# Local attention scores with a block diagonal of keys in four column tiles, and row steps queued one task later

## The chip, the core and the metric

The kernel runs on one core of a Trainium2 chip. A core has TensorE (matrix products, PE in the profile, with its weight loads listed apart as PEld), VectorE (DVE), ScalarE (ACT), GpSimd (POOL) and SyncE (SP), and 16 DMA engines. The metric is the device time of one execution in microseconds; a kernel's time is the median of its runs.

## What is computed

A masked attention over 8 batches of 8 heads, 576 positions, 64 channels, followed by a mixture of 8 experts of which each token uses one. The first four heads see the last 32 positions (local), the others every 32nd position (strided).

```python
mask_local = (rel >= 0) & (rel < stride)
mask_strided = (rel >= 0) & (pos[None, :] % stride == pos[:, None] % stride)
scores = np.where(masks[None, :, :, :], scores, -1000000000.0)
attn = softmax(scores)                      # over the last axis
x = (attn @ v).transpose(0, 2, 1, 3).reshape(B * S, H * D)
expert = argmax(x @ w_gate); gate = softmax(x @ w_gate)[expert]
out = gate * (relu(x @ w1[expert]) @ w2[expert])
```

## The kernel before

**Attention.** Each batch is cut into five tasks (`BANK_PAIRS`), 40 in all. A task fills one PSUM bank of 128x512 scores. Tasks 0 and 1 of a batch hold the local scores of two heads each, for 16 blocks of 32 queries; tasks 2 to 4 hold the rest of the local scores and the strided ones. `stage_s` writes a mask into the bank by a matmul with the identity (line 403), adds the scores (lines 411, 419, 424), and `softmax` runs over the bank on VectorE, ScalarE and GpSimd (lines 352 to 362). Three tasks later `stage_t` transposes the probabilities (line 453), and four tasks later `av_local` (line 478) and `av_strided` (line 467) multiply them with the values; ScalarE copies the results to `xT` (line 162).

**Local scores.** A block of 32 queries of two heads meets 64 keys. Before, the queries stand as a block diagonal in `qkl` (head 0 in rows 0 to 63, head 1 in rows 64 to 127, zeros between). `wide` takes the 64 columns of a block as the weights, with a step of 16 elements, and 64 keys as the moving side; the result is 64 rows of 64 columns, and two column tiles are used in turn:

```python
q = qkl[k][:, 0:2 * LQ].rearrange("p (q j) -> p q j", j=LB)
nc.tensor.matmul(sb[64 * i:64 * i + 64, col:col + 64], q[:, :, j], qkl[k][:, k0:k0 + 64],
                 start=False, stop=last, tile_position=(0, 64 * i))
```

Every fp32 matmul of the program is two instructions in the trace, each with a weight load of its own.

**Row steps.** When a batch's last values are made, `row_steps` lists what follows for its rows: the logits of three row tiles at a time (`logits`: line 528, a copy `ls` to SBUF on VectorE at line 158, transposes at line 535, small work on VectorE), the rows' transposes and their store to DRAM (`xrows`, line 520), and after every second batch the routing (`route`). The list goes into `queue`, and `step()` takes one piece; an iteration of the task loop calls `step()` four times, twice ahead of `stage_s` and twice behind the values. `row_steps` puts one empty piece (`pause`) ahead of the logits.

**Early experts.** After the fourth batch's routing, `fillers()` starts windows of 256 rows of experts 0, 2, 4 and 6; `filling()` takes one piece of them twice in an iteration. A window gathers its rows (line 239), transposes them (line 275), splits weights into a high and a low part (ScalarE line 222, VectorE line 223) and multiplies (lines 297 to 299, 286 to 288). What is left of them comes behind the loop. Then the eight experts follow, with three small remainders (`small`, lines 1031 and 1043) whose matmuls have 32 columns of weights, 128 moving columns and four column tiles.

**What sets the order.** On TensorE the order is the program's own (`manual_schedule`). On the other engines a scheduler sets it from priorities. Loads of queries, keys and values are issued by SyncE, in its order, when the buffer is free; a local task's `qkl` has one buffer, freed when the scores of the batch before are done.

Of the kernel before, what the change touches and what calls it, by code (L numbers as in the profile page):

```python
# [22 lines left out]
QB = 32  # L23
# [93 lines left out]
def host_constants(np):  # L117
# [3 lines left out]
    for p in range(128):  # L121
        q = p % QB
        m[p, 0, q + 1:q + QB + 1] = 0.0
        m[p, 1, max(q + 1, QB if p < 2 * QB else 0):q + QB + 1] = 0.0
# [19 lines left out]
def moe_attn(ctx, tc, qk, vv, wg, wcat, blob0, blob, out):  # L144
# [175 lines left out]
    with ExitStack() as actx:  # L320
# [13 lines left out]
        def make_masks():  # L334
            for k, kinds in enumerate((((0, 1, 1), (1, 8, 0)), ((0, 2, 0), (2, 8, 2)), ((0, 8, 2),))):
# [31 lines left out]
        qkl = [loc.tile([128, 2 * LQ + LK], F32, name=f"qkl{k}") for k in range(2)]  # L367
        pTl = [loc.tile([128, 2, 512], F32, name=f"pTl{k}") for k in range(2)]
        for k in range(2):
            nc.vector.memset(qkl[k][64:128, 0:LQ], 0.0)  # L370
            nc.gpsimd.memset(qkl[k][0:64, LQ:2 * LQ], 0.0)
# [4 lines left out]
        def load_qk(i):  # L376
            if i < len(tasks):
                b, k = tasks[i]
                if k < 2:
                    o = QKO[k]  # L380
                    nc.sync.dma_start(out=qkl[k][64:128, LQ:], in_=qk[b, 64:128, o:o + LQ + LK])
                    nc.sync.dma_start(out=qkl[k][0:64, 0:LQ], in_=qk[b, 0:64, o:o + LQ])
                    nc.sync.dma_start(out=qkl[k][0:64, 2 * LQ:], in_=qk[b, 0:64, o + LQ:o + LQ + LK])
                    return
# [15 lines left out]
        def stage_s(b, k):  # L400
# [7 lines left out]
            def wide(j, i, col, last):  # L408
                q = qkl[k][:, 0:2 * LQ].rearrange("p (q j) -> p q j", j=LB)
                k0 = 2 * LQ + QB * j  # L410
                nc.tensor.matmul(sb[64 * i:64 * i + 64, col:col + 64], q[:, :, j], qkl[k][:, k0:k0 + 64],  # L411
                                 start=False, stop=last, tile_position=(0, 64 * i))
# [14 lines left out]
            for n, (kind, hp, m) in enumerate(BANK_PAIRS[k]):  # L427
                for y in range(2):
                    col = 128 * n + 64 * y
                    last = n == 3 and y == 1  # L430
                    if kind == "l":
                        for i in range(2):
                            wide(4 * m + 2 * i + y, i, col, last)
                    elif kind == "lx":
# [34 lines left out]
        def av_local(b, xT, off):  # L469
            for hp in range(2):  # L470
                av = bank("v")
                for m in range(4):
                    for i in range(2):
                        n = 2 * m + i
                        vt = v_of(b, hp, "l", n)
# [320 lines left out]
        def row_steps(g, bb, xT, L):  # L796
# [422 lines left out]
```

## Time and profile before

| | us |
|---|---|
| median of three runs | 666.14 |
| lowest, highest | 664.89, 667.58 |
| profiled execution | 671.04 |
| its span on the core | 668.8 |

The rows of the section below come from that profiled execution; times are from the span's start. In a row by stretch, each engine's busy time is followed by the number of its instructions in brackets, then come the granted clock of TensorE as a share, the mean busy share of the DMA engines, and GB/s. A row of a group gives the line, the engine, the operation, output<-inputs, shapes, the count, the busy time, and the mean of one in ns. A row of the timeline gives start, length, engine, line and count, and in square brackets the idle time ahead of it with what ended it. Matmuls are pipelined: the time from the start of one group to the start of the next is what it holds TensorE, the busy time of one is longer by its tail.

### The profile page before, as it was taken

The numbers are of one execution on the slowest core, as the hardware profiler recorded it, in microseconds if no ns is written. First come the engines' busy times: TensorE is split into PE (matmuls) and PEld (weight loads), VectorE is DVE, ScalarE is ACT, GpSimd is POOL, SyncE is SP. The second block draws the span as 40 slices with busy tenths as digits, with TensorE's granted clock in tenths as the row PEclk, the third lists the DMA queues.
The fourth block names the chain that finished last, engine by engine and source line by source line (L and its number), as shares of the span: only waits on it lengthen the run. The fifth ranks groups of instructions, "written<-read, shape, count | busy, mean of one in ns | idle before, by whom it ended". The sixth has DMA issues, their size and how long they took to land.

```text
span 668.8 us, 14979 instructions
## 1 busy us (share of the span) xinstructions
PE 626.7 (94%) x6136; PEld 522.0 (78%) x6154; DVE 400.9 (60%) x788; ACT 327.3 (49%) x584; POOL 148.1 (22%) x168
## 2 busy tenths in 40 slices
PE   4999889789979999999899899999999999999996
PEld 3877778577858778888588788887898788887885
DVE  5667968656757369899424576823596235863332
ACT  1556665565645565356332555622565224753232
POOL 3232223420041021216100413200612004301021
PEclk9899999989989999899999999999999999999999
DMA  9968998994652865558933576872896546863301
GB/s 283 243 231 270 299 302 256 333 342 162 222 212 96 300 225 167 179 193 280 384 142 117 204 292 209 282 252 92 314 356 219 170 181 225 328 238 150 126 20 64
DMA packets 36550, 149.85 MB, mean 224 GB/s; under 512 B 5114, under 2 KB 5504, under 8 KB 26240
## 3 DMA queue, kind: packets, MB, share of 16 engines
q1 hardware_dynamic: 22848, 105.92, 47.1%
q10 hardware_dynamic: 7344, 22.70, 9.5%
q0 software_dynamic: 6288, 20.26, 8.3%
q8 instruction: 49, 0.80, 0.5%
q14 instruction: 21, 0.17, 0.1%
HBM read 129.69 MB, written 19.63 MB: 223 GB/s over the span
## 4 chain that ended last, share of the span: by engine, by line
PE 35%; issue 34%; POOL 7%; DMA 5%; DVE 4%; ACT 2%; POOLq 1%; ACTq 0%; another core or an unknown queue 0%
POOL xg L239 4%; PE t L297 4%; PE t L299 4%; PE t L298 4%; PE y L286 4%; PE y L287 3%; PE y L288 3%; POOL out_dram L258 2%; PE s L411 2%; DMA raw<-in_wcat_dram 1%; PE v L520 1%; DMA out_dram<-y,oids 1%; PE v L467 1%; DMA xg<-xd,eids 1%; DMA xd<-xr 1%
## 5 line engine op out<-in xcount | busy, mean ns | idle before, releaser
L223 DVE TENSOR_TENSOR wlo<-raw,whi 128x1024 fp32r<-128x1024 f32 x136 | 164.0, 1222 | 76.2 <-ACT whi L222 68.1
L222 ACT CAST whi<-raw 128x1024 fp32r<-128x1024 f32 x136 | 139.3, 1051 | 63.4 <-PE s L288 25.4
L297 PE MATMUL t<-xh,whi 128*128 128x256 f32 (+1 forms) x384 | 126.9, 332 | 2.3 <-ACT xh L231 2.1
L298 PE MATMUL t<-xl,whi 128*128 128x256 f32 (+1 forms) x384 | 124.3, 324 | 0.0
L299 PE MATMUL t<-xh,wlo 128*128 128x256 f32 (+1 forms) x384 | 123.6, 322 | 0.5 <-DVE wlo L223 0.5
L303 DVE SCALAR_TENSOR_TENSOR hl<-t,hh 128x256 fp32r<-128x256 f32 (+1 forms) x96 | 49.0, 510 | 103.2 <-ACT hh L302 102.9
L302 ACT ACTIVATE hh<-t 128x256 fp32r<-128x256 f32 (+1 forms) x96 | 43.8, 456 | 120.7 <-PE t L299 109.2
L297 PEld LDWEIGHTS t<-xh,whi 128*128 128x128 f32 x384 | 73.1, 191 | 13.3 <-ACT xh L231 3.3
L286 PE MATMUL y<-whi,hh 128*128 128x512 f32 x192 | 77.2, 402 | 2.1 <-ACT hh L302 2.1
L299 PEld LDWEIGHTS t<-xh,wlo 128*128 128x128 f32 x384 | 73.6, 192 | 6.3 <-DVE wlo L223 1.1
L298 PEld LDWEIGHTS t<-xl,whi 128*128 128x128 f32 x384 | 73.4, 191 | 5.9 <-DVE xl L232 0.3
L287 PE MATMUL y<-wlo,hh 128*128 128x512 f32 x192 | 75.9, 395 | 0.0
L288 PE MATMUL y<-whi,hl 128*128 128x512 f32 x192 | 74.6, 395 | 0.0
L362 POOL TENSOR_TENSOR prob<-prob,ri 128x512 f32<-128x512 f32 x40 | 42.5, 1063 | 122.9 <-DVE ri L361 87.6
L258 POOL DMA_INDIRECT out_dram<-y,oids x24 | 27.5, 1147 | 115.7 <-DVE y L257 110.9
L162 ACT COPY xT<-v 128x270 f32<-128x270 f32 (+1 forms) x80 | 30.1, 480 | 28.8 <-PE v L467 12.3
L286 PEld LDWEIGHTS y<-whi,hh 128*128 128x128 f32 x192 | 36.4, 189 | 9.4 <-ACT hh L302 2.9
L288 PEld LDWEIGHTS y<-whi,hl 128*128 128x128 f32 x192 | 35.9, 189 | 9.1 <-DVE hl L303 1.3
L287 PEld LDWEIGHTS y<-wlo,hh 128*128 128x128 f32 x192 | 36.5, 190 | 5.0
L358 DVE TENSOR_REDUCE sm<-prob 128x8 f32<-128x512 f32 x40 | 27.3, 683 | 21.5 <-ACT prob L356 21.2
L352 DVE TENSOR_REDUCE nm<-s 128x8 f32<-128x512 f32 x40 | 27.3, 683 | 18.5 <-PE s L411 14.0
L239 POOL DMA_INDIRECT xg<-xd,ids x24 | 30.2, 1259 | 31.9 <-ACT xh L231 18.9
(219 smaller groups left out, 1056.7 us busy)
## 6 DMA issues: line engine op xcount, KB each, us to landing
raw<-in_wcat_dram SPq DMA_DIRECT2D x68, 1024.0 KB
sraw<-in_wcat_dram ACTq DMA_DIRECT2D x12, 1024.0 KB
xd<-xr ACTq DMA_DIRECT2D x36, 264.0 KB
vl<-in_vv_dram SPq DMA_DIRECT2D x16, 512.0 KB
qkl<-in_qk_dram SPq DMA_DIRECT2D x16, 264.0 KB
vt<-in_vv_dram SPq DMA_DIRECT2D x16, 256.0 KB
qk<-in_qk_dram SPq DMA_DIRECT2D x8, 484.0 KB
qk<-in_qk_dram SPq DMA_DIRECT2D x8, 432.0 KB
```

The lines of the kernel that those rows point to most:

```text
L222: nc.scalar.copy(out=hi[:, sl], in_=raw[:, sl])
L223: i = nc.vector.tensor_tensor(out=lo[:, sl], in0=raw[:, sl], in1=hi[:, sl].bitcast(F32), op=ALU.subtract)
L239: lastp[0] = nc.gpsimd.indirect_dma_start(out=xg, out_offset=None, in_=xd[0:rows, :], in_offset=bass.IndirectOffsetOnAxis(ap=idc, axis=0))
L286: nc.tensor.matmul(yb[t], hh[:, ts], whi[:, w], start=(j == 0), stop=False)
L287: nc.tensor.matmul(yb[t], hh[:, ts], wlo[:, w], start=False, stop=False)
L288: nc.tensor.matmul(yb[t], hl[:, ts], whi[:, w], start=False, stop=(j == 7))
L297: nc.tensor.matmul(hb[:, 0:n], whi[:, w], xh[:, dc, :], start=(dc == 0), stop=False)
L298: nc.tensor.matmul(hb[:, 0:n], whi[:, w], xl[:, dc, :], start=False, stop=False)
L299: nc.tensor.matmul(hb[:, 0:n], wlo[:, w], xh[:, dc, :], start=False, stop=(dc == 3))
L302: nc.scalar.activation(out=hh[:, 0:n], in_=hb[:, 0:n], func=AF.Relu)
L303: nc.vector.scalar_tensor_tensor(out=hl[:, 0:n], in0=hb[:, 0:n], scalar=0.0, in1=hh[:, 0:n].bitcast(F32), op0=ALU.max, op1=ALU.subtract)
L362: lastp[0] = nc.gpsimd.tensor_tensor(out=pv, in0=pv, in1=ri.unsqueeze(2).broadcast_to([128, 8, 64]), op=ALU.mult)
```

## The change

Three things change.

- In `wide`, the 32 queries of both heads are the weights, as 32 contiguous columns, and the keys are the block diagonal on the moving side: two runs of 64. The result is 32 rows of 128 columns, written as two runs of 64 columns, in four column tiles. The mask, the loads into `qkl` and the host's layout follow it.
- Since the blocks stand in another order in the bank, `av_local` reads other columns of the probabilities and writes two runs of 32 columns in place of one of 64. It has as many matmuls as before.
- The list of `row_steps` goes into `late`, and from there into `queue` in the next task; the last batch's list goes into `queue` at once. The empty piece is gone.

```diff
-                    nc.sync.dma_start(out=qkl[k][64:128, LQ:], in_=qk[b, 64:128, o:o + LQ + LK])
-                    nc.sync.dma_start(out=qkl[k][0:64, 0:LQ], in_=qk[b, 0:64, o:o + LQ])
-                    nc.sync.dma_start(out=qkl[k][0:64, 2 * LQ:], in_=qk[b, 0:64, o + LQ:o + LQ + LK])
+                    nc.sync.dma_start(out=qkl[k][0:64, 0:LQ + LK], in_=qk[b, 0:64, o:o + LQ + LK])
+                    nc.sync.dma_start(out=qkl[k][64:128, 0:LQ], in_=qk[b, 64:128, o:o + LQ])
+                    nc.sync.dma_start(out=qkl[k][64:128, LQ + LK:], in_=qk[b, 64:128, o + LQ:o + LQ + LK])
...
-            def wide(j, i, col, last):
-                q = qkl[k][:, 0:2 * LQ].rearrange("p (q j) -> p q j", j=LB)
-                k0 = 2 * LQ + QB * j
-                nc.tensor.matmul(sb[64 * i:64 * i + 64, col:col + 64], q[:, :, j], qkl[k][:, k0:k0 + 64],
-                                 start=False, stop=last, tile_position=(0, 64 * i))
+            def wide(m, i, last):
+                j = 4 * m + i
+                keys = qkl[k][:, LQ:].rearrange("p (h x) -> p h x", h=2)[:, :, QB * j:QB * j + 64]
+                o = sb[QB * i:QB * i + QB, 256 * (m // 2):256 * (m // 2) + 256].rearrange("p (h y c) -> p h y c", h=2, y=2)
+                nc.tensor.matmul(o[:, :, m % 2], qkl[k][:, QB * j:QB * j + QB], keys,
+                                 start=False, stop=last, tile_position=(0, QB * i))
...
-                            c = 128 * m + 64 * i + 32 * h
-                            nc.tensor.matmul(av[64 * h:64 * h + 64, 64 * n:64 * n + 64], vt[:, 64 * h:64 * h + 64],
+                            c = 128 * (2 * m + h) + QB * i
+                            o = av[64 * h:64 * h + 64, 256 * m:256 * m + 256].rearrange("p (y r) -> p y r", y=2)
+                            nc.tensor.matmul(o[:, :, QB * i:QB * i + QB], vt[:, 64 * h:64 * h + 64],
                                              pTl[hp][:, :, c:c + QB], start=True, stop=True, tile_position=(0, 64 * h))
...
-            pause = [] if last else [single()]
-            steps = list(pause)
+            steps = []
             for r in range(3):
                 steps += [part(x) for x in lg]
-                if r == 0:
-                    steps += pause
...
-                    if k == 1:
+                    if k == 0:
+                        queue.extend(late)
+                        late.clear()
+                    elif k == 1:
...
-                        queue.extend(row_steps(g, bb, xTs[g], Ls[g]))
+                        (queue if b == B - 1 else late).extend(row_steps(g, bb, xTs[g], Ls[g]))
```

TensorE, from the last strided values of the second batch on. Before (a row is a run of equal instructions; `t` are transposed probabilities, `s` scores, `v` values, `y` the bank of logits and rows):

```order
L467 MATMUL v<-pT,vt 64x54 x20
L467 MATMUL v<-pT,vt 64x36 x4
L528 MATMUL y<-xT,wg_sb 32x384 x4
L453 MATMUL t<-cst_70,prob 128x128 x4
L528 MATMUL y<-xT,wg_sb 32x384 x4
L535 MATMUL y<-cst_70,ls 128x128 x3
L403 LDWEIGHTS identb
L403 MATMUL s<-mask_b,identb 128x512
L424 MATMUL s<-qk 54x54 x16
L535 MATMUL y<-cst_70,ls 128x128 x3
L453 MATMUL t<-cst_70,prob 128x128 x4
```

The same place of the changed kernel, whose lines stand two further down here (467 is 469, 528 is 530, 535 is 537):

```order
L469 MATMUL v<-pT,vt 64x54 x20
L469 MATMUL v<-pT,vt 64x36 x4
L455 MATMUL t<-cst_70,prob 128x128 x4
L403 LDWEIGHTS identb
L403 MATMUL s<-mask_b,identb 128x512
L425 MATMUL s<-qk 54x54 x16
L530 MATMUL y<-xT,wg_sb 32x384 x8
L455 MATMUL t<-cst_70,prob 128x128 x4
L537 MATMUL y<-cst_70,ls 128x128 x6
```

Both groups of logits moved behind the next task's transposes, mask and scores, and their transposes follow together.

SyncE, ahead of the first load of expert weights (`raw`), with the last loads of a batch in front of it. Before:

```order
L387 DMA qk<-in_qk_dram 128x864
L394 DMA vt<-in_vv_dram 128x512
L214 DMA raw<-in_wcat_dram 128x2048
L381 DMA qkl_135<-in_qk_dram 64x1056
L382 DMA qkl_135<-in_qk_dram 64x512
```

In the changed kernel, at the same place:

```order
L387 DMA qk<-in_qk_dram 128x864
L394 DMA vt<-in_vv_dram 128x512
L381 DMA qkl_135<-in_qk_dram 64x1056
L382 DMA qkl_135<-in_qk_dram 64x512
L383 DMA qkl_135<-in_qk_dram 64x544
L394 DMA vl<-in_vv_dram 128x1024
```

The load of weights moved behind the 14 loads of one more batch, of which the rows show the first four.

## Rows read from the trace of the kernel before

**Rows 1.** The page: busy time and share of the span by engine.

```profile
PE 626.7 (94%) x6136; PEld 522.0 (78%) x6154; DVE 400.9 (60%) x788; ACT 327.3 (49%) x584; POOL 148.1 (22%) x168
```

**Rows 2.** Busy time by stretch: PE, PEld, DVE, ACT, POOL, clock, DMA share, GB/s.

```profile
0.00:22.00 22.00, 13.20 (x183) 10.19 (x184) 11.41 (x33) 6.04 (x9) 7.67 (x15) 0.84 0.96 273
22.00:42.00 20.00, 19.02 (x384) 14.39 (x383) 14.90 (x37) 11.59 (x25) 6.63 (x9) 1.00 0.81 247
42.00:61.50 19.50, 18.96 (x389) 14.20 (x389) 12.91 (x33) 11.23 (x26) 5.31 (x6) 1.00 0.83 259
61.50:83.40 21.90, 20.11 (x417) 16.78 (x419) 19.39 (x57) 14.46 (x31) 6.14 (x11) 1.00 0.87 278
83.40:104.50 21.10, 19.14 (x391) 14.71 (x393) 14.34 (x36) 13.02 (x29) 5.39 (x8) 1.00 0.92 296
104.50:125.70 21.20, 19.23 (x416) 16.29 (x417) 17.92 (x59) 14.49 (x31) 6.85 (x12) 1.00 0.91 292
125.70:137.00 11.30, 7.54 (x113) 6.09 (x113) 4.01 (x14) 3.49 (x8) 6.57 (x9) 1.00 1.03 320
...
400.00:668.00 268.00, 263.49 (x1727) 220.59 (x1725) 133.68 (x169) 119.14 (x195) 49.80 (x41) 1.00 0.57 203
```

**Rows 3.** TensorE's matmuls grouped by line and shape.

```profile
L411 PE MATMUL s<-qkl 128*64 128x64 f32 x512 | 33.2, 289 | 2.7 <-DMA qkl<-in_qk_dram 1.6 <-issue 0.7
...
L478 PE MATMUL v<-pTl,vl 128*64 128x64 f32 x512 | 17.7, 223 | 1.9 <-issue 1.9
...
L1031 PE MATMUL v<-sraw,sxt 128*32 128x128 f32 x192 | 6.5, 276 | 0.0
...
L419 PE MATMUL s<-qk 64*32 64x64 f32 x128 | 3.4, 222 | 0.3 <-DMA xd<-xr 0.2
```

**Rows 4.** TensorE's weight loads grouped by line and shape.

```profile
L411 PEld LDWEIGHTS s<-qkl 128*64 128x64 f32 x512 | 30.8, 209 | 7.1 <-issue 6.5 <-DMA vl<-in_vv_dram 0.3 <-DMA qk<-in_qk_dram 0.3
...
L1031 PEld LDWEIGHTS v<-sraw,sxt 128*32 128x32 f32 x192 | 4.9, 109 | 2.1 <-issue 2.1
```

**Rows 5.** TensorE's timeline at the end of the second batch's values.

```profile
54.66 1.76 PE L528 MATMUL y<-xT,wg_sb 128*32 128x384 f32 x6
...
57.34 0.66 PE L453 MATMUL t<-cst,prob 128*128 128x128 f32 x4
57.93 0.85 PE L528 MATMUL y<-xT,wg_sb 128*32 128x384 f32 x8
58.71 0.55 PE L535 MATMUL y<-cst,ls 128*128 128x128 f32 x3
59.40 1.01 PE L424 MATMUL s<-qk 64*54 64x54 f32 x32
```

**Rows 6.** The same place after the first, third, fourth and fifth batch.

```profile
35.37 1.69 PE L528 MATMUL y<-xT,wg_sb 128*32 128x384 f32 x6
...
37.99 0.66 PE L453 MATMUL t<-cst,prob 128*128 128x128 f32 x4
...
79.03 2.16 PE L528 MATMUL y<-xT,wg_sb 128*32 128x384 f32 x8
81.83 0.55 PE L535 MATMUL y<-cst,ls 128*128 128x128 f32 x3 [0.65 <-DVE ls L158]
...
97.25 0.84 PE L528 MATMUL y<-xT,wg_sb 128*32 128x384 f32 x4
...
100.35 0.66 PE L453 MATMUL t<-cst,prob 128*128 128x128 f32 x4
...
122.59 1.37 PE L528 MATMUL v<-xT,wg_sb 128*32 128x384 f32 x8 [0.59 <-ACT xT L162]
```

**Rows 7.** Timeline: first scores, first load of expert weights, first expert matmul.

```profile
6.85 2.12 PE L411 MATMUL s<-qkl 128*64 128x64 f32 x32 [1.60 <-DMA qkl<-in_qk_dram]
...
83.19 0.33 SPq L214 DMA_DIRECT2D raw<-in_wcat_dram  x1
...
141.74 0.37 PE L297 MATMUL t<-xh,whi 128*128 128x256 f32 x1
```

More of the change, by code (lines that the diff above doesn't have):

```diff
@@ L123, in host_constants @@
         m[p, 0, q + 1:q + QB + 1] = 0.0
-        m[p, 1, max(q + 1, QB if p < 2 * QB else 0):q + QB + 1] = 0.0
+        m[p, 1, max(q + 1, QB if p < QB else 0):q + QB + 1] = 0.0
         r, a = divmod(p % 64, SR)
@@ L334, in make_masks @@
         def make_masks():
-            for k, kinds in enumerate((((0, 1, 1), (1, 8, 0)), ((0, 2, 0), (2, 8, 2)), ((0, 8, 2),))):
+            for k, kinds in enumerate((((0, 8, 0), (0, 1, 1), (2, 3, 1)), ((0, 2, 0), (2, 8, 2)), ((0, 8, 2),))):
                 for x0, x1, m in kinds:
@@ L365, in moe_attn @@
         loaded = {}
-        qkl = [loc.tile([128, 2 * LQ + LK], F32, name=f"qkl{k}") for k in range(2)]
+        qkl = [loc.tile([128, LQ + 2 * LK], F32, name=f"qkl{k}") for k in range(2)]
         pTl = [loc.tile([128, 2, 512], F32, name=f"pTl{k}") for k in range(2)]
         for k in range(2):
-            nc.vector.memset(qkl[k][64:128, 0:LQ], 0.0)
-            nc.gpsimd.memset(qkl[k][0:64, LQ:2 * LQ], 0.0)
+            nc.vector.memset(qkl[k][64:128, LQ:LQ + LK], 0.0)
+            nc.gpsimd.memset(qkl[k][0:64, LQ + LK:], 0.0)
         for k in range(2):
@@ L427, in stage_s @@
             for n, (kind, hp, m) in enumerate(BANK_PAIRS[k]):
+                if kind == "l":
+                    for i in range(4):
+                        wide(m, i, m == 3)
+                    continue
                 for y in range(2):
@@ L430, in stage_s @@
                     last = n == 3 and y == 1
[L431 to L434, printed above, removed]
+                    if kind == "lx":
                         for i in range(2):
@@ L471, in av_local @@
                 av = bank("v")
[L472 to L475, printed above, removed]
+                for m in range(2):
+                    for i in range(4):
+                        vt = v_of(b, hp, "l", 4 * m + i)
                         for h in range(2):
-                            c = 128 * m + 64 * i + 32 * h
-                            nc.tensor.matmul(av[64 * h:64 * h + 64, 64 * n:64 * n + 64], vt[:, 64 * h:64 * h + 64],
+                            c = 128 * (2 * m + h) + QB * i
+                            o = av[64 * h:64 * h + 64, 256 * m:256 * m + 256].rearrange("p (y r) -> p y r", y=2)
+                            nc.tensor.matmul(o[:, :, QB * i:QB * i + QB], vt[:, 64 * h:64 * h + 64],
                                              pTl[hp][:, :, c:c + QB], start=True, stop=True, tile_position=(0, 64 * h))
@@ L777, in moe_attn @@
         queue = []
+        late = []
         def run(gen):
@@ L1140, in host_layout @@
     for j in range(NQB):
-        vl[:, j % 2, :, :, j // 2] = vp[:, :, QB * j:QB * j + 64, :].reshape(B, 2, 2, 64, D).transpose(0, 3, 1, 2, 4)
+        y, n = (j // 4 % 2, 4 * (j // 8) + j % 4) if j < LB else (j % 2, LB // 2)
+        vl[:, y, :, :, n] = vp[:, :, QB * j:QB * j + 64, :].reshape(B, 2, 2, 64, D).transpose(0, 3, 1, 2, 4)
     vl = vl.reshape(B, 128, 2, NQB // 2, 128)
@@ L1163, in host_layout @@
                 parts = [lq[:, k, :, 0:LQ], lk[:, k, :, 0:LK]]
-                parts[0] = parts[0].reshape(B, 128, LB, QB).transpose(0, 1, 3, 2).reshape(B, 128, LQ)
             elif key[0] == "lx":
```

## Prediction

> **What bounds the kernel now.** I read the page's busy shares first, then the busy time of each engine by stretch, then TensorE's groups by shape, and last the timeline where TensorE pauses. TensorE is busy 626.7 of 668.8 us, and no other engine is above 60% [rows 1]. The stretches say where that matters: from 400 us to the end it is busy 263.5 of 268 us, so whatever ends earlier before that point ends earlier at the end, too [rows 2]. From 22 to 125.7 us, the five batches of attention that run without expert work beside them, TensorE is busy 18.96 of 19.5 to 20.11 of 21.9 us per batch [rows 2], so it is the bound there. Two others stand close behind it: the DMA engines at 0.81 to 0.92 of the time, and VectorE, which is busy 19.39 of 21.9 us in the batch that also routes [rows 2]. A gain on TensorE in this stage is worth its full size only until one of these two is full.
>
> **Scores of the local heads.** Every fp32 matmul of the program is two instructions in the trace: 16 local tasks of 16 matmuls give the 512 of line 411. They take 33.2 us, 64.8 ns each, while line 478, with the same 128x64 weights and 64 moving columns, takes 17.7 us for its 512, 34.6 ns each [rows 3]. What differs is the weight load: 209 ns against 109 ns for 32 columns in a row [rows 4]; line 411 reads its 64 columns with a step of 16 elements. The changed line has 32 contiguous columns of weights, 128 moving columns and four column tiles taken in turn. Lines 1031 and 1043 of the expert tail have that shape: line 1031 takes 6.5 us for 192, which is 33.9 ns [rows 3]. So 512 x (64.8 - 33.9) = **15.8 us** less on TensorE, 0.99 us per task, twice per batch. The bounds are 64.8 ns, no gain, if the four tiles don't run side by side here, and 26.6 ns (line 419, 32-column weights and half the moving columns: 3.4 us for 128 [rows 3]), which would be 19.6 us. I take line 1031, whose weights, columns and tiles are the same; that two runs of keys are read instead of one costs nothing by line 478, whose moving side is already two runs of 32. A loss on the reading side is excluded, because no more columns stream per tile than there.
>
> **What the written side costs.** Both local lines now write their result in two runs (64 columns in line 412 of the changed kernel, 32 in line 480) instead of one. No matmul row of the trace writes two runs, so the cost is open: from 0 (the reading side of line 478) to a doubling, 34.6 ns for each of the 512 of line 478, or 17.7 us. I take 0, since the runs are long, and keep the doubling as a rival.
>
> **The order of the row steps.** Before, the first logits of a batch (line 528) stand right behind the last strided values (line 467), two copies of which ScalarE has not yet made. The timeline shows line 528 in pieces, from 54.66 to 57.34, where line 453 starts; eight instructions without a wait take 0.78 us, from 57.93 to 58.71 [rows 5]. That wait is 1.90 us. The other batches, by the same reading [rows 6]: 2.62 - 0.78 = 1.84 at 35.37; 2.80 - 0.78 = 2.02 at 79.03, up to line 535; 3.10 - 0.78 = 2.32 at 97.25; and 1.37 - 0.85 = 0.52 at 122.59, both busy times. Later batches have expert matmuls in between, and the last is not moved. The sum is 8.6 us. In the changed order a transpose of probabilities (0.59 us from 57.34 to 57.93), a mask and 32 score instructions (1.01 us busy at 59.40) come first [rows 5], some 1.9 us with the mask, about what the copies need. What is late next is line 535: in the first and third batch it follows line 528 directly, and waits for the copy `ls` in between; 81.83 shows 0.65 us of that wait [rows 6], twice 1.3 us. That leaves **7.3 us**. The bounds are 0, if the wait moves on to line 453, and 8.6.
>
> **What else moves.** The first expert's weights stand behind one more batch of loads in SyncE's queue; today they are issued at 83.19 and the first expert matmul runs at 141.74 [rows 7], so the 21 us of one batch are covered. Two of the expert steps leave the attention loop and come behind it. TensorE does them there at the same cost, and the stretch behind is TensorE-bound, so 0; the order of the gathers on GpSimd moves with them, one iteration later, where TensorE had idled 3.8 us anyway, from 125.70 on [rows 2]. The four score instructions of a column tile need the first mask in three casts instead of two; TensorE then waits 1.60 us for the keys in any case [rows 7], which covers it. The loads keep their sizes, and each memset grows by a sixteenth.
>
> **The sum and what caps it.** On TensorE 15.8 + 7.3 = 23.1 us, of which 4 tasks x 0.99 = 4.0 us lie behind 125.7 us. The other 19.1 lie before it, and there the DMA engines have work of their own: 0.96 x 22 + 0.81 x 20 = 37.3 us, 16.2 + 19.1 = 35.2, and 19.4 + 19.3 = 38.7, together 111.2 us [rows 2]. So 125.7 can shrink to 111.2 at the least, by 14.5 us rather than 19.1. VectorE's 32.3 us of 41.4 in the pair from 42 to 83.4 leave it just inside. 14.5 + 4.0 = **18.5 us**. The profiled execution is 671.0 us (span 668.8), so it would be 652.5; it lies 4.9 above the median of 666.1, and for the median I predict 647.6, rounded to **648 us**.
>
> **Rivals.**
> Loads hold the stage: the highest share that the DMA engines reached over a batch while TensorE kept going is 0.92 [rows 2]. If that is full, 125.7 shrinks to 111.2 / 0.92 = 120.9, and the gain is 4.8 + 4.0 = 8.8: 657 us. For it speaks that the loads of a batch wait for the buffer that the batch before frees. Against it, that the one wait for keys in the rows is the first, 1.60 us at the start [rows 7]. 0.20.
> The moved steps bring nothing, because line 453 then waits for its probabilities (VectorE, 32.3 of 41.4 us busy, has little room to run ahead): 15.8 us, 650 us. 0.13.
> Nothing caps it, and the pause after 125.7 us (11.3 - 7.5 = 3.8 us [rows 2]) mostly goes: 23.1 + 3 = 26, 640 us. 0.12.
> The column tiles don't overlap and line 412 stays at 64.8 ns: 7.3 us, 659 us. 0.07.
> Slower: the writes in two runs cost twice. Line 480 then takes 17.7 us more, line 412 goes to 67.8 ns, 1.5 more than now, and the moved steps give 7.3 back: +11.9, 678 us. It turns to a loss from 23.1 us / 1024 instructions = 22.6 ns per instruction on. Against it speaks that both lines keep runs of 128 bytes and more. 0.06. The Trainium skill has a rule for this, in PSUM — Partial Sum Buffer, Specifications (TRN2): PSUM is read and written in lines of 8 bytes, and any access pattern with gaps slows matmuls significantly. By that rule this rival would be the result; no row of the trace before shows such a write, so it is neither borne out nor refuted there.
>
> **How the numbers follow.** 0.42 for the forecast, with 0.20, 0.13, 0.12, 0.07 and 0.06 for the rivals in their order. The range 640 to 659 takes in all but the slower one and the far ends of the forecast's neighbours, about 0.15 left out. A measurement of this kernel tells about 0.5% (3.3 us) from no change, so faster means under 662.8: all cases but the last, less a little for the cases at 657 and 659 coming out weaker: 0.90, 0.05 within, 0.05 slower.
>
> **What would show it.** Line 412 should read near 17 us for 512, with weight loads near 109 ns; line 480 should stay at 17.7 us, and more than 25 would mean the write rival. Line 530 should stand in one piece of 0.85 us; a wait of line 455 for GpSimd would mean that the stall only moved. The first 125 us should end some 14 us earlier with a DMA share near 1; a share that stays at 0.9 with TensorE waiting for keys or values would mean that the loads hold it. The prediction is wrong if TensorE's work falls by 16 us and the end moves by less than 7.

## The result and the profile after

| | before | after |
|---|---|---|
| median, us | 664.91 | 674.14 |
| lowest, highest, us | 661.12, 667.58 | 668.01, 684.95 |
| runs | 12 | 12 |
| span of the profiled execution, us | 668.8 | 672.8 |

The ratio after to before is 1.0113, with a 95% interval of 1.008 to 1.0147: the changed kernel is 1.1% slower, where 648 us, 2.7% faster, had been predicted. The ratio leaves out three of the 12 runs after that lie over 1.5% above the fastest (679.04 us and more). The kernel before is about 5 us slower in its profiled execution than in its median. Those 5 us have a place: between the 192nd and the 256th matmul of line 299 it needs 106.3 us, where the changed kernel and eleven of the fifteen experiments below need 101 (`k1_after_warm` needs 106.4, too). Why it does was not found. Seen from the median, then, the traces differ by 9 us at the end, as the medians of all runs do, not by the 4 of the spans.

TensorE has less to do. The page of the changed kernel, its groups of TensorE matmuls and weight loads by shape (output<-inputs, shapes, count | busy us, mean ns | idle before), and a piece of its timeline where nothing waits (start, length, engine, line, count):

```profile
span 672.8 us, 15008 instructions
PE 620.0 (92%) x6154; PEld 512.7 (76%) x6154; DVE 404.3 (60%) x789; ACT 325.8 (48%) x584; POOL 148.2 (22%) x168
```

```profile
L412 PE MATMUL s<-qkl 128*32 128x128 f32 x512 | 20.3, 304 | 1.6 <-DMA qkl<-in_qk_dram 1.3 <-issue 0.4
L480 PE MATMUL v<-pTl,vl 128*64 128x64 f32 x512 | 18.6, 237 | 0.0
...
L412 PEld LDWEIGHTS s<-qkl 128*32 128x32 f32 x512 | 15.1, 121 | 8.9 <-issue 7.3 <-DMA qk<-in_qk_dram 0.8 <-DMA vt<-in_vv_dram 0.6
```

```profile
54.90 1.71 PE L530 MATMUL y<-xT,wg_sb 128*32 128x384 f32 x16
56.54 0.66 PE L455 MATMUL t<-cst,prob 128*128 128x128 f32 x4
...
58.70 1.08 PE L412 MATMUL s<-qkl 128*32 128x128 f32 x32
59.71 2.08 PE L480 MATMUL v<-pTl,vl 128*64 128x64 f32 x64
61.73 0.44 PE L455 MATMUL t<-cst,prob 128*128 128x128 f32 x2
```

Line 412 takes 20.3 us where line 411 took 33.2, and a weight load 121 ns where it took 209 [rows 3, 4]. From the start of one group to the next, 32 matmuls of line 412 hold TensorE for 59.71 - 58.70 = 1.01 us, 31.6 ns each. Line 480 holds it for 2.02 us for 64, where line 478 held it for 1.96 at the same clock: the writes in two runs cost next to nothing. The second batch's logits, which stood in pieces [rows 5], now stand in one piece of 16, from 54.90 to 56.54.

The end did not follow. Busy time by stretch of the changed kernel, the stretches from 22 us on those of [rows 2] (engines' busy time with instructions in brackets, then TensorE's granted clock, DMA share, GB/s):

```profile
22.00:42.00 20.00, 17.32 (x384) 13.11 (x383) 13.77 (x38) 11.85 (x26) 6.27 (x7) 0.83 0.92 269
42.00:61.50 19.50, 18.87 (x483) 15.11 (x477) 14.48 (x40) 12.14 (x28) 7.05 (x12) 1.00 0.80 250
61.50:83.40 21.90, 18.99 (x430) 14.72 (x426) 17.56 (x54) 14.29 (x31) 7.12 (x11) 1.00 0.94 298
83.40:104.50 21.10, 17.55 (x400) 13.15 (x399) 13.82 (x43) 11.90 (x28) 5.87 (x10) 1.00 0.94 304
104.50:125.70 21.20, 17.93 (x408) 14.01 (x407) 18.31 (x48) 14.74 (x31) 6.32 (x7) 0.92 0.94 325
125.70:137.00 11.30, 6.65 (x79) 4.41 (x77) 8.49 (x17) 6.25 (x13) 7.04 (x10) 0.88 0.99 282
```

TensorE is no longer full there: 17.5 to 18 of 21 us in the last batches, where it was 19.1 to 19.2 [rows 2]. The DMA engines, at 0.81 to 0.92 in these batches before, are at 0.92 to 0.94 in four of the five. The clock, 1.00 in these batches before, is at 0.83 and 0.92 in two of them. The local scores that stood at 125.70 start at 121.43, so 4.3 us were gained there, and from then on some 13 us were lost, as seen from the medians. This is what TensorE waited for from 22 to 245 us (engine, output, line, what came last: us in total, times, longest):

```profile
PE v L275 <- ACT xr L162: 6.4, 4, 3.9
PE y L620 <- DVE bb L613: 3.0, 1, 3.0
PE v L522 <- DVE xl L232: 2.6, 1, 2.6
PE v L537 <- DVE ls L158: 2.1, 1, 2.1
PE y L537 <- DVE ls L158: 2.1, 4, 0.7
PE v L275 <- ACT xT L162: 1.9, 2, 1.1
PE v L469 <- issue: 1.7, 1, 1.7
PE t L455 <- issue: 1.7, 1, 1.7
PE y L574 <- issue: 1.7, 1, 1.7
PE y L530 <- issue: 1.6, 2, 1.3
```

The waits sit at three kinds of places: where a row step now follows its producer too closely (lines 537 and 620), where a row step and an expert's transposes want the same PSUM bank `v` (lines 275 and 522), and "issue", where TensorE had no instruction. The longest one, in the timelines of TensorE, GpSimd and ScalarE:

```profile
128.29 0.66 PE L522 MATMUL v<-cst,xT 128*128 128x128 f32 x4
128.78 0.60 PE L455 MATMUL t<-cst,prob 128*128 128x128 f32 x4
129.28 0.66 PE L522 MATMUL v<-cst,xT 128*128 128x128 f32 x4
133.84 0.94 PE L275 MATMUL v<-cst,xg 128*128 128x128 f32 x2 [3.90 <-ACT xr L162]
```

```profile
124.71 1.07 POOL L239 DMA_INDIRECT xg<-xd,eids  x1 [4.64 <-DMA raw<-in_wcat_dram]
126.09 0.97 POOL L239 DMA_INDIRECT xg<-xd,eids  x1 [0.31 <-PE v L480]
127.08 1.05 POOL L362 TENSOR_TENSOR prob<-prob,ri 128x512 f32<-128x512 f32 x1
128.28 0.98 POOL L239 DMA_INDIRECT xg<-xd,eids  x1 [0.16 <-issue]
129.57 0.96 POOL L239 DMA_INDIRECT xg<-xd,eids  x1 [0.31 <-DVE gt L552]
130.55 1.05 POOL L362 TENSOR_TENSOR prob<-prob,ri 128x512 f32<-128x512 f32 x1
131.53 1.48 POOL L519 COPY xr<-gt 128x16 f32<-128x16 f32 x3
```

```profile
133.20 0.59 ACT L162 COPY xr<-v 128x512 f32<-128x512 f32 x1 [3.02 <-POOL xr L519]
```

Read from the bottom: ScalarE empties bank `v` only when GpSimd has written the gates (line 519). GpSimd has four gathers and two softmax products ahead of that. TensorE's next transposes need the bank, and stand until 133.84. What the clock does behind such pauses is seen in these stretches:

```profile
134.30:144.50 10.20, 8.81 (x118) 7.33 (x119) 5.86 (x13) 6.18 (x14) 1.76 (x2) 0.50 0.87 293
185.50:195.70 10.20, 7.63 (x99) 6.54 (x100) 7.60 (x15) 4.02 (x8) 2.58 (x3) 0.50 0.73 231
```

```profile
187.47 1.12 PE L522 MATMUL v<-cst,xT 128*128 128x128 f32 x4 [2.65 <-DVE xl L232]
188.38 1.06 PE L455 MATMUL t<-cst,prob 128*128 128x128 f32 x4
```

For 10.2 us after the pause that ends at 133.84, and for 10.2 us around the one that ends at 187.47, TensorE was granted 1.2 of its 2.4 GHz. The same four transposes of line 522 hold it for 188.38 - 187.47 = 0.91 us there, and for 0.49 at 128.29.

### The profile page after: what moved, and what is told of

Read it like the earlier page. It is cut to its first block, busy times and chain, and to the rows that moved or that the text cites. A ratio compares the mean times of both kernels' runs of the same rounds, so it can differ in the third digit from the quotient of the medians.

```text
span 672.8 us, 15008 instructions
## 1 busy us (share of the span) xinstructions
PE 620.0 (92%) x6154; PEld 512.7 (76%) x6154; DVE 404.3 (60%) x789; ACT 325.8 (48%) x584; POOL 148.2 (22%) x168
## 4 chain that ended last, share of the span: by engine, by line
PE 57%; issue 4%; DMA 2%; POOL 2%; ACT 1%; DVE 1%; POOLq 0%; ACTq 0%; another core or an unknown queue 0%
PE t L297 7%; PE t L299 7%; PE t L298 7%; PE y L286 5%; PE y L288 5%; PE y L287 5%; PE s L286 2%; PE s L287 2%; PE s L288 2%; PE v L275 1%; DMA out_dram<-y,oids 1%; POOL xg L239 1%; PE s L973 1%; PE t L955 1%; PE t L956 1%
## 5 line engine op out<-in xcount | busy, mean ns | idle before, releaser
L223 DVE TENSOR_TENSOR wlo<-raw,whi 128x1024 fp32r<-128x1024 f32 x136 | 165.7, 1236 | 76.3 <-ACT whi L222 76.1
L286 PEld LDWEIGHTS y<-whi,hh 128*128 128x128 f32 x192 | 36.6, 191 | 11.3 <-ACT hh L302 5.2
L162 ACT COPY xT<-v 128x270 f32<-128x270 f32 (+1 forms) x80 | 30.8, 473 | 28.6 <-PE v L469 14.2
```

The costliest lines, as they stand in the source:

```text
L223: i = nc.vector.tensor_tensor(out=lo[:, sl], in0=raw[:, sl], in1=hi[:, sl].bitcast(F32), op=ALU.subtract)
L286: nc.tensor.matmul(yb[t], hh[:, ts], whi[:, w], start=(j == 0), stop=False)
```

## Experiments

Three theories went in. First, the later list is to blame, and without it the shorter scores reach the end. Second, with shorter scores TensorE is no longer what bounds the attention stage, so that little can arrive whatever the order. Third, the pauses pull TensorE's clock down, and this costs by itself. The kernels were compared with the kernel before in runs of the same sitting; since 664.98 to 671.87 us was measured for the latter, the ratios are to be read, not the medians.

### One half of the change at a time

`e1_diag` has the block diagonal and the old order, `e2_late` the old scores and the later list.

Against the changed kernel, `e1_diag` is:

```diff
-            steps = []
+            pause = [] if last else [single()]
+            steps = list(pause)
...
-                        (queue if b == B - 1 else late).extend(row_steps(g, bb, xTs[g], Ls[g]))
+                        queue.extend(row_steps(g, bb, xTs[g], Ls[g]))
```

> The block diagonal in four column tiles alone: the row steps enter the queue as in the kernel before, with the pause. Theory 1, the later list is what costs (it starts the expert work one task later, and puts the gathers and row steps behind one another): without it the 13 us that TensorE's scores give reach the end, and the time is 650 to 655 us, ratio 0.98. Theory 2, TensorE is no longer the bound of the attention stage once its scores are shorter, so that only little of the 13 us can arrive whatever the order: 662 to 668 us, ratio 0.995 to 1.005, with more pauses of TensorE ('issue', loads, softmax chains) in the place of the work. Theory 3, the pauses let TensorE's clock fall to half, which costs what the shorter scores gain: ratio 0.995 or above, and more stretches at a granted clock of 0.5 than the kernel before has.

Measured: 660.60 us, ratio 0.9926 (0.9893 to 0.9958).

> The later list alone: scores, tiles and layout of the kernel before, the row steps one task later, without the pause. Theory 1: slower by 1 to 3%, 672 to 685 us, since nothing makes up for it; about 24 us above the block diagonal alone. Theory 2: it moves the 7 to 8 us of the stall at line 528 to other places and the time stays within 0.5%, or gains up to 5 us. Theory 3: as many half-clock stretches as the changed kernel and slower by about 1%, if the pauses that the later list makes are the cause; as few as the kernel before and no slower, if the shorter scores make them.

Measured: 674.54 us, ratio 1.0119 (1.0048 to 1.0189).

The later list alone is as slow as the whole change, which the first theory had said; but without it the shorter scores bring 0.7%, not the 2% of the first theory. That lies just below the 0.995 or above of the second and the third. `e2_late` speaks against the second, which had put it within 0.5%, and the third alone does not explain it: `e2_late` is as slow as the change with 14 us at half clock from 110 to 245 us, as much as `e1_diag` has, where the change has 27. The stretch of the five attention batches shows what became of the gain in `e1_diag`. This is the row for 22 to 125 us of the kernel before, and then that of `e1_diag`:

```profile
22.00:125.00 103.00, 95.75 (x1985) 75.99 (x1992) 79.48 (x218) 64.10 (x137) 30.32 (x44) 1.00 0.87 274
```

```profile
22.00:125.00 103.00, 90.32 (x1985) 66.63 (x1992) 79.01 (x219) 64.34 (x138) 30.26 (x44) 0.95 0.89 279
```

The same 1985 matmuls were done in the same 103 us, with 5.4 us less busy time at a clock of 0.95: what the shorter scores saved came back as pauses and slower matmuls. The local scores at 125.7 start at 125.1 in `e1_diag` and at 119.4 in `e2_late`, so in its trace the later list brings 6.3 us up to there, and loses them and more behind. In all these kernels a late list is also one without the empty piece; the two were not told apart.

### Fewer loads

`e3_after_vonce` (the changed kernel), `e4_before_vonce` (the kernel before) and `f3_diag_vonce` (the block diagonal alone) load the values of the first batch only.

```diff
                 b, k = tasks[i]
+                if b > 0:
+                    loaded[b, "v", k] = loaded[0, "v", k]
+                    return
```

> The changed kernel, but the values of the first batch serve all batches: the loads of vl and vt are left out for the other seven, 1.9 of some 4.3 MB a batch (so the attention output is computed with other values). Theory 2, the loads hold the attention stage: 14 us or more faster than the changed kernel, 660 us or less, and the batches from 22 to 125 us at 17 us or less each. Theory 1: no more than 3 us faster, 671 us. Theory 3: the gain depends on whether the half-clock stretches go: with the same number of them it stays above 668 us.

> The control: the kernel before with the values of the first batch for all batches (the same loads left out). All theories: TensorE bounds the kernel before in the attention stage, so at most 3 us faster than the kernel before, ratio 0.995 to 1.0. If it is faster by 1% or more, the loads hold the kernel before, too, and the stage was not TensorE's in the first place.

> The block diagonal alone, with the values of the first batch for all batches (the other loads of values are left out, so that the attention is computed with other values and the experts get other rows: only the first 125 us can be compared). If the loads are what keeps the gain of the shorter scores from arriving: the sixth pair of local tasks starts at 112 to 116 us, against 125 with the loads, since the kernel before without these loads needed 124.2. If the order of the row steps and the pauses hold it, and not the loads: 121 or later.

Measured: 786.05, 787.73 and 776.47 us in all, the last from one run. These totals say nothing, and the first two expectations were wrong to give any: with other values other rows go to the experts, and the end of the program grows. The attention stage can be read, by the start of the same local scores as above:

| start of those scores, us | all loads | values once | difference |
|---|---|---|---|
| before | 125.7 | 124.2 | 1.5 |
| block diagonal alone | 125.1 | 116.0 | 9.1 |
| changed kernel | 121.4 | 111.4 | 10.0 |

With fewer loads the block diagonal brings 124.2 - 116.0 = 8.2 us. TensorE's part is 9.4 us: ten tasks from 22 us on at 1.95 - 1.01, where 1.95 is the middle of the 1.85 to 2.03 us that 32 matmuls of line 411 held it for in this stage. So most of it arrives; with all loads 0.6 us of it does. Each of these starts is one trace, and `g3_diag_wait6` below, whose code is that of `e1_diag` up to the early experts, has the scores at 120.0 us, so that 5.7 us arrive there. The row of `f3_diag_vonce` for the same stretch, at a DMA share of 0.78 and a clock of 0.98:

```profile
22.00:125.00 103.00, 91.64 (x2093) 70.06 (x2095) 82.60 (x229) 68.63 (x146) 37.56 (x53) 0.98 0.78 238
```

So the loads keep a part of the gain of the shorter scores from arriving: without them these scores come 4.0 to 9.1 us earlier with the block diagonal, and 1.5 us earlier in the kernel before, held by TensorE. How they do it is not shown by TensorE's waits: from 22 to 121 us the changed kernel waits 12.8 us in all, none of it for a load, and 7.1 us of it with "issue", without an instruction.

### Where the later list costs

`f1_late012` has the changed kernel's later list for the first three batches only, `f2_late_not3` for all but the fourth, the one whose list routes and starts the expert work (there `LATE` is 0, 1, 2, 4, 5, 6).

```diff
+        LATE = (0, 1, 2)
...
+            pause = [] if last or g * GB + bb in LATE else [single()]
...
-                        (queue if b == B - 1 else late).extend(row_steps(g, bb, xTs[g], Ls[g]))
+                        (late if b in LATE else queue).extend(row_steps(g, bb, xTs[g], Ls[g]))
```

> The changed kernel, with the later list only for the first three batches; from the fourth on, whose list also routes and starts the expert work, the list enters the queue as in the kernel before. The theory after the first runs: the later list costs where expert work and row steps share TensorE, since there the row steps come out at other pieces of it and TensorE pauses for gathers and copies; ahead of it the list brings 5 to 6 us, of which the shorter scores add little. Then the first 83 us keep the gain of the changed kernel (3.5 us and more), the expert work starts some 3 us or more earlier than in the kernel before, and the whole is 655 to 661 us, ratio 0.985 to 0.992. The rival, that the loads alone set the stage and no order helps: the same as the block diagonal alone, 0.9926. If the later list costs in the first batches too, it is above 0.996.

Measured: 658.67 us, ratio 0.9896 (0.9839 to 0.9953).

> The changed kernel with the later list for all batches but the fourth, so that the expert work starts at its old place and the lists of batches five to seven come late. If what costs is that the expert work starts one task later, so that two of its pieces leave the loop: as fast as with the later list for the first three batches alone, 655 to 661 us. If what costs is that the late lists meet other pieces of the expert work: 668 to 674 us, ratio 1.005 to 1.012, with TensorE's pauses between 180 and 250 us as long as in the changed kernel, against some 9 us less without.

Measured: 660.64 us, ratio 0.9909 (0.9878 to 0.994).

Nearly the whole loss hangs on one list out of seven: with the fourth in its old place the change gains 0.9%. `f1_late012` has the lowest ratio of the study, though its interval overlaps with those of `e1_diag` and `f2_late_not3`. In its attention stage the same scores start at 116.8 us, 8.9 earlier than before (119.9 in `g1_fill`, whose code is the same up to there), and the DMA engines are at 0.96:

```profile
22.00:125.00 103.00, 88.72 (x2089) 69.81 (x2092) 80.26 (x227) 65.81 (x142) 33.24 (x48) 0.99 0.96 300
```

Then it, too, gives some back, at the first expert's transposes, which wait for the gathered rows:

```profile
129.62 0.45 PE L275 MATMUL v<-cst,xg 128*128 128x128 f32 x1 [8.27 <-DMA xg<-xd,eids]
131.00 0.90 PE L275 MATMUL v<-cst,xg 128*128 128x128 f32 x3 [0.93 <-DMA xg<-xd,eids]
```

### Is it the gather, or the place of the expert's pieces?

The fourth list does two things when it is late: its gather is issued a task later, and the expert's pieces stand a task later among the attention tasks and row steps. `g3_diag_wait6` and `g4_wait6` move only the pieces (in `e1_diag` and `f1_late012`), `h1_not3_wait6` does so in `f2_late_not3`.

```diff
             cur = make(EXP[0])
-            for _ in range(4):
+            for _ in range(6):
                 yield
```

> The block diagonal alone (660.6 us), with the early experts' first transposes two pieces, one task, further behind the gather. Nothing else moves: the lists stay where they are. If the loss of the changed kernel comes from the expert work starting one task later (two of its pieces leave the loop, and those left meet other row steps): slower by 5 to 13 us, 666 to 673 us. If it comes from the late lists themselves, and a later first transpose only fills the pause at 129 us with attention: as fast or up to 5 us faster, 656 to 661 us.

Measured: 668.13 us, ratio 0.9969 (0.9944 to 0.9994).

> The later list for the first three batches alone (658.7 us), again with the first transposes one task further behind the gather. If pauses and the clock behind them set the loss: the pause of 8.6 us and the half-clock stretch of 10.2 us behind it go, the eighth expert group comes no later than 144 us with one more task of attention done by then, and the time is 652 to 657 us. If pieces that leave the loop cost: 663 to 670 us, with the sixty-fourth group 6 us and more later than 217.7.

Measured: 667.78 us, ratio 0.995 (0.9914 to 0.9986).

> The changed kernel with the fourth batch's list in its old place (ratio 0.991), and the first transposes of the early experts one task further behind their gather: the pieces then stand on TensorE where the changed kernel has them, while the gather is issued a task earlier. If the late gather is what costs: ratio 0.993 to 0.999, the eighth expert group near 142 to 143 us. If the place of the pieces costs: ratio 1.005 or above, and the pauses from 180 to 250 us as in the changed kernel.

Measured: 676.23 us, ratio 1.0151 (1.0098 to 1.0203).

| | pieces at their old place | pieces one task later |
|---|---|---|
| lists of batches 5 to 7 at once | 0.9896 (`f1`) | 0.995 (`g4`) |
| lists of batches 5 to 7 late | 0.9909 (`f2`) | 1.0151 (`h1`), 1.0113 (the change) |

Each move alone costs 0.1 and 0.5%, which the intervals do not tell apart; both together cost 2.2 to 2.6%, which they do. `e2_late` has both, too, with the old scores, at 1.0119. The gather of `h1` does not wait for a late list, and `h1` is as slow as the change. That alone does not clear the gather: in the trace of `h1` the attention stage is 4 us behind that of `f2_late_not3`, whose code is the same up to there (the scores start at 124.7 us instead of 120.6), and the first gather comes no earlier than the 124.71 us of the change. But in `e1_diag`, at a ratio of 0.9926, it comes later still. The first gather of `h1`, and then that of `e1_diag`:

```profile
125.14 1.47 POOL L239 DMA_INDIRECT xg<-xd,eids  x1 [1.28 <-DMA vt<-in_vv_dram]
```

```profile
127.34 1.07 POOL L239 DMA_INDIRECT xg<-xd,eids  x1 [3.67 <-DMA qk<-in_qk_dram]
```

So a late gather does not make a kernel slow by itself. What costs is late lists and late pieces together. The waits tell only part of it. These are the longest of `h1` from 121 to 250 us, and then those of `f2_late_not3`:

```profile
PE v L522 <- ACT xT L162: 5.3, 1, 5.3
PE v L537 <- DVE ls L158: 3.1, 2, 2.1
PE v L522 <- DVE xl L232: 2.7, 1, 2.7
```

```profile
PE v L522 <- ACT xT L162: 5.3, 1, 5.3
PE v L522 <- DVE xl L232: 2.3, 1, 2.3
PE v L537 <- DVE ls L158: 1.6, 2, 1.4
```

The places are the same, and a row step's wait for the bank `v` behind an expert's transposes is in both; line 537 waits 1.5 us longer in `h1`. The clock differs more: from 110 to 245 us it is at 0.91 in `h1`, and at 0.96 in `f2_late_not3` and `f1_late012`.

Two more kernels drain the queue faster until the expert work starts, `h2_late012_quick` from `f1_late012` and `h3_after_quick` from the changed kernel.

```diff
                 step()
                 filling()
                 step()
+                if ia >= EG * GB * NBK - 1 and not fill:
+                    step()
+                    step()
```

> The later list for the first three batches alone (ratio 0.99), with two more steps of the queue in each task from the end of the fourth batch's values until the expert work starts, so that the fourth list runs out one to two tasks earlier. If the first gather is the point that the middle of the kernel hangs on: the gather is issued 4 us or more before 120.3 us, the pause of 8.6 us ahead of the first transposes shrinks, the eighth group comes at 136 to 139 us, and the ratio is 0.980 to 0.986. If TensorE or the loads are the bound there: the same 0.99, or above it because the row steps wait for VectorE.

Measured: 664.03 us, ratio 1.0003 (0.9971 to 1.0036).

> The changed kernel, all lists late, with the same two more steps of the queue in each task between the fourth batch's values and the start of the expert work. If the late gather is what costs: it is issued at 117 to 121 us (124.7 in the changed kernel), and the ratio falls from 1.011 to 0.99 to 0.998. If the late lists of batches five to seven, or the place where row steps meet expert pieces, cost: 1.005 or above even with an early gather.

Measured: 665.14 us, ratio 1.0023 (0.9992 to 1.0055).

`h2` issued its first gather at 118.97 us instead of 120.29, less than expected, and lost 1% against `f1`: the faster row steps push the attention tasks back (the scores that start at 116.8 us in `f1` start at 135.7), and the loop's last transposes of probabilities come at 231.1 us instead of 214.8. So nothing here shows that an earlier gather is worth anything by itself. `h3` wins 0.9% back for the change; it puts the pieces earlier again, so it speaks for the place as much as for the gather, and alone would not have told them apart.

### The clock

`f4_diag_fill`, `g1_fill` and `k1_after_warm` put transposes of the identity, whose result is overwritten or never read, where TensorE stood idle.

For `k1_after_warm`, with four calls of it at the places that its expectation names:

```diff
+        def warm(n, tag=None, t=None):
+            t = bank(tag) if t is None else t
+            for _ in range(n):
+                nc.tensor.transpose(t[:, 0:128], ident, ident)
```

> The block diagonal alone, with eight transposes of the identity (about 1.2 us) ahead of the logits of the first four batches, into the bank that the logits then overwrite: TensorE works where it waited for the copies of the values, and its clock has less reason to fall. If the falls of the clock cost what the shorter scores gain, 3 us or more: no stretch at 0.5 between 22 and 125 us, and 656 to 659 us, below the block diagonal alone (660.6). If the pauses themselves cost and not the clock: the same 660 us within 2. If the transposes come on top (TensorE does not wait there any more): 4 to 7 us slower, 665 us.

Measured: 666.16 us, ratio 1.0034 (0.9999 to 1.0069).

> The changed kernel with the later list for the first three batches alone, and 48 transposes of the identity (some 7 us at the full clock) ahead of the first transposes of the early experts' rows, where TensorE stood idle for 8.6 us before it ran at half its clock for 10.2 us. If the fall of the clock behind a pause costs by itself: no half-clock stretch there, the expert work from its eighth group on 3 to 5 us earlier than without the transposes, and 653 to 656 us. If the pause alone costs and the clock is no matter (the engine then waits for gathers and copies, not for itself): the eighth group at the same 141.9 us and the same 658.7 us. If the gathered rows come sooner than 7 us: later by the rest.

Measured: 663.45 us, ratio 0.9914 (0.9883 to 0.9945).

> The changed kernel with transposes of the identity where TensorE stood idle ahead of a half-clock stretch: 18 ahead of line 620 (it waited 3.0 us for bb), 28 ahead of the first early expert's transposes (3.9 us for a bank), 16 ahead of the row transposes at 187.5 us (2.6 us for a bank), 14 ahead of line 537 at 208.9 us (2.1 us for ls); 2.0, 3.1, 1.8 and 1.5 us at the 0.11 us of one, so less than each wait, and nothing else is changed. If the falls of the clock cost by themselves: the stretches at 0.5 between 110 and 245 us (27 us in the changed kernel) shrink to 10 us or less, and the time falls by 4 us or more, ratio 0.996 to 1.006. If only the pauses cost: the half-clock stretches go and the time stays, 1.009 or above. If the stretches at half clock stay, the test says nothing.

Measured: 673.79 us, ratio 1.003 (0.9999 to 1.0061), against 1.0113 without the transposes. The rows for 110 to 245 us, of the changed kernel and then of `k1_after_warm`:

```profile
110.00:245.00 135.00, 115.93 (x1540) 94.42 (x1531) 85.06 (x195) 72.89 (x146) 32.89 (x45) 0.90 0.67 224
```

```profile
110.00:245.00 135.00, 118.40 (x1606) 99.22 (x1611) 86.15 (x208) 72.95 (x147) 32.21 (x44) 0.97 0.70 233
```

The time at half clock in this stretch falls from 27 to 7 us, the mean clock rises from 0.90 to 0.97, and 0.8% of the time comes back, about 5.5 us of the 13 that separate the change from `f2_late_not3`. Not all of that is the clock's for certain: in the traces `k1` is 5.7 us ahead at the 192nd matmul of line 299, and 2.2 of these stand there ahead of the first added transposes (the same four of line 455 start at 113.81 us in `k1` and at 115.97 in the change). So the third theory holds for 3.5 to 5.5 us. Nor does the time at half clock put the kernels in order: `h3` has 24 us of it in this stretch at a ratio of 1.0023, `e2_late` 14 at 1.0119. The two other fills show the limits. `g1_fill` took the idling out of the longest pause, and with it the 10.2 us at half clock behind it; the eighth group of the expert came at 141.5 instead of 141.9 us, and the ratio is that of `f1_late012` within the intervals; since its scores had started 3.1 us later than those of `f1`, ahead of the fill, the traces do not tell what the fill is worth. The 48 transposes took 5.3 us, not the 7 that were expected, and the expert's own followed them without a wait: they ran at full clock, but began later, at 132.35 instead of 129.62 us. `f4_diag_fill` put work ahead of the logits whether TensorE would have waited or not, and was 1% slower than without: idle time that differs from batch to batch can't be filled by a fixed number.

## Why the prediction was wrong

**The size of the shorter scores was right.** 15.8 us had been worked out from line 1031; line 412 came to 20.3 us, 12.9 less than line 411 [rows 3], and to 31.6 ns each at the full clock, against the 33.9 that were taken from busy time, the tail included; where the clock is at half, as at 121.43, 32 of them take 1.87 us in place of 1.01. The four column tiles do overlap.

**The written side costs what was taken, next to nothing.** Line 480 went from 17.7 [rows 3] to 18.6 us. The Trainium skill says, in PSUM — Partial Sum Buffer, Specifications (TRN2), that access patterns with gaps slow matmuls significantly; for runs of 32 and 64 fp32 columns the runs here do not bear that out: 2.02 us for 64 matmuls with two runs of 32 against 1.96 with one run of 64, and 1.08 us busy for 32 matmuls with two runs of 64 (at 58.70) as for 32 of line 1031 with one run (at 634.57 in the trace before). The slower rival had its sign right and its mechanism wrong.

**The order of the row steps** was taken at 7.3 us, and brings 6.3 in the trace of `e2_late` up to the scores at 125.7. Up to there this step held, as far as one trace tells.

**The first step that failed is the cap.** The sum let the stage shrink until the DMA engines would be full, 111.2 us, a gain of 14.5. They reach 0.91 over the stage in the changed kernel, 0.96 in the best variant, and the scores come at 121.4 and 116.8 us: the stage gains 4.3 us in the change, not 14.5. The rival "loads hold the stage" took the highest share that had been seen [rows 2] for full and gave 120.9; that was the right number for the stage, at a chance of 0.20. Its mechanism is borne out in part. Leaving the values out showed that the loads matter: 8.2 of 9.4 us arrive then, against 0.6 and 5.7 in two traces with all loads. But the sign that had been named for it, TensorE waiting for keys or values, did not come: its longest waits in this stage are for row steps and for instructions. Why the DMA engines stop short of full was not tried.

**The step that turned the sign is "what else moves".** It was put at nothing, and the one list that starts the expert work costs 2.0% when it comes late (`f2_late_not3` against the change), some 13 us. Two pieces of the expert work were said to leave the loop at no cost, because the stretch behind it is TensorE-bound, and the gathers to move into 3.8 us that are idle anyway [rows 2]. Moving the pieces alone costs 0.4 to 0.5% (`g3` against `e1`, `g4` against `f1`), moving the late lists beside the expert work alone 0.1%, all within the intervals, and both together more than 2%. No term of the sum asked which row step would come to stand next to which piece of the expert work, or right behind its own producer. The list of waits after names both kinds: lines 522 and 275 on bank `v`; line 537 right behind the copy it needs, line 620 behind VectorE's `bb`. The row 125.70 to 137.00, with 7.54 us of work in 11.3 [rows 2], had been read as a place to hide things; it was a sign that TensorE waits for others there.

**The clock was in no term.** It had stood at 1.00 in all five attention batches [rows 2]. Once TensorE pauses for 2 to 4 us in the places above, it falls to half, and 3.5 to 5.5 us go, by `k1_after_warm`.

**What was right in the list of signs:** line 412 (20.3 us for the 17 that were named), its weight loads (121 ns for 109), line 480 and the logits in one piece came nearly as written, and so did the sign for a failure: TensorE's scores fell by 12.9 us of 16, and the end moved the other way. The sign for the stage, some 14 us at a DMA share near 1, did not come.

**Open:** of the 13 us between the change and `f2_late_not3`, 3.5 to 5.5 are the clock by `k1_after_warm`. TensorE's waits from 22 to 250 us, added up, are 28.6 us in the change and 25.7 in `f2_late_not3`, 3 us more. The other 5 to 7 were not located; the 7 us at half clock that `k1` left in place, and work that is left behind the loop without shortening it, are candidates. That the clock stays at half for 10.2 us around the wait of 2.6 us in the change, and for 3.4 us around one of 2.7 us in `e2_late`, was not explained.

## What to carry to other kernels

Shorter work on the busiest engine is worth what the next resource leaves of it: take the highest share that this resource has shown while the busiest engine kept going (here 0.92 over a batch) as full, not 1.00, and make that the forecast rather than a rival. When an order is changed, list which instruction comes to stand next to which for every list that moves, the PSUM bank and the queue (here GpSimd's) that both need, and move the lists in groups, to see which of them lose; here the kernel with three of seven late was 1.0% faster than before, and one of the others lost 2%. Where TensorE was no longer full here it also lost its clock, so that a pause cost more than its length.

## What the hardware showed

**A pause costs twice.** Four transposes of line 522 held TensorE for 0.49 us at the full clock and 0.91 us at half, and the changed kernel spent 27 us of the stretch from 110 to 245 us there. Work whose result nobody reads, placed where the engine would have stood, gave back up to 0.8%.

**TensorE can run out of instructions.** "Issue" waits of 1.1 to 4.0 us appear in the attention stage of the kernels with shorter scores and all loads, except `g3_diag_wait6` and `f4_diag_fill` (0.6 and 0.4 at most), 7.1 us from 22 to 245 us in the changed kernel; with the old scores, before and in `e2_late`, the longest was 0.6. One of them, in the changed kernel, ahead of line 469:

```profile
33.66 0.68 PE L469 MATMUL v<-pT,vt 54*64 54x54 f32 x33 [1.72 <-issue]
```

It ends 1.5 us after a packet of the instruction queue (q8) has landed, at 32.17 us, and the others of the changed kernel end 1.4 to 1.6 us after one, too. With the values loaded once the longest is 0.6 us. That the loads delay the instructions is suggested by this, not shown. The waits also differ without a cause in the code: programs whose code is the same up to the early experts differ by up to 5 us in the start of the scores there, 125.1 in `e1_diag` against 120.0 in `g3_diag_wait6`. So the 0.6 us that arrive with the block diagonal alone are one trace's, and the 8.2 without the loads another's; the medians, 0.7% for the block diagonal, are the safer reading.
